# Later additions, a later read of finished chains, and new slot orders in a kernel that mixes a Fourier layer with attention

## The chip, the cores and the metric

The kernel runs on one core of one Trainium2 chip. The metric is the device time of one execution in microseconds (us); of several runs the median is taken.

## The reference

Input x is 2048 x 512 in float32. Two branches of it are mixed by a gate:

```
# Fourier branch
a, b = x @ dft_hid_re.T, x @ dft_hid_im.T
y    = dft_seq_re @ a - dft_seq_im @ b                    # 2048 x 2048 times 2048 x 512, twice
# attention branch: 32 heads of width 16
q, k, v = split(x @ wqkv)
o = softmax(q @ k.T * 16**-0.5) @ v                       # per head, 2048 x 2048 scores
out_b = o @ wo
# gate
g = sigmoid((x * gate_w).sum(-1))
out = g * y + (1 - g) * out_b
```

## The kernel before

Matrix products that need accuracy are split in a high and a low part and done as three products (high x high, high x low, low x high); this is what `h1` and `l1` mean. Heads go in pairs p = 0 to 15 (`NP`).

**Scores.** Each head's scores are computed twice. An `a` tile (`a_tile`, line 217) has queries in rows and 512 keys in columns; VectorE reduces it to row maxima (line 219, `mx`). When the maxima of half a pair (1024 queries) are complete, two deferred steps follow, one at the end of each of the next two sections: `m_parts` (lines 228 to 232: maxima negated on VectorE, split into `nhl` on GpSimd) and `m_rows` (lines 236 to 240: VectorE transposes them to `mt`, and eight small transfers, four issued on SyncE and four on GpSimd, write them as two further rows of the pair's query stack `qs`). An `s` tile (`scores`, line 682) has keys in rows and 512 queries in columns; with those rows the maximum is subtracted in the product, and ScalarE writes its exponential (line 683, `pt`). So `a` tiles run ahead of `s` tiles.

**Values.** A unit u is 128 keys of one pair and one half of the queries; there are 512 units (`UNITS`). `pv` (line 708) takes two units: eight products with `vt` (line 718, which the profile counts as sixteen instructions) into one accumulator. ScalarE copies it to `oe`, of which there are two buffers, and GpSimd adds `oe` to the running sum `osum` (lines 727 and 728; the first of a group of eight is copied straight to `osum`, line 724). After the group's last, two transfers on SyncE write the sum to `o_d` (line 731). From there `sums` (line 478), `inverse` (lines 484 to 489), `load_o` and `block` make normalised, split blocks for the projection.

**Chains.** The Fourier products and the projections are chains of products into one PSUM bank of their own (`psD`, `d` in the profile, line 378). A chain's last product has a function `after` that reads the bank: `real_next` (line 394, ScalarE copies to `y`, GpSimd splits it into `xab`), `dft_next` (lines 432 and 435, ScalarE; GpSimd adds; SyncE stores), `proj_next` (line 559 in `finish`, VectorE). `dft_next` also issues the split of a later chunk of the sequence matrix (`c_split`, lines 333 and 334 on GpSimd) and its load (line 323), in the last round of the first half reloads `xab` from `b_d` (line 428), and in the last round of all loads `wo_hl` and `o_hl` (lines 462 and 468).

**Sections.** The order of TensorE's work is written out by hand. In the long middle stretch products and scores use half the rows of the array each: a section with `half` 0 runs chain products on rows 0 to 63 and scores on rows 64 to 127, and the next section, `half` 1, the other way round; the two go through the same products, so a product is complete after both. A pattern lists a section's slots. A slot of one letter is one chain product beside one score tile of that kind on the other half. A slot of two letters has no product: the first letter is a tile on the other half, the capital one a tile on the product's half. `|` is the value product. There are three kinds:

- THIN, 26 sections, with the hidden-axis products (12 a section);
- FULL, 192 sections, with the sequence-axis products (16 a section);
- NINE, 26 sections in pairs of two different patterns, with projections (9 a section).

Before them stands a short start, after them a tail with an order of its own. The two halves have a stream of tiles each (stream 0 and stream 1).

The first product of a section that continues a chain waits, by a dependency that is added by hand, for a reader of the tiles issued since the last product of the section before: the last exponential among them, else the first reduction (`before` in `segment`).

Scores and accumulators share seven PSUM banks. `bank` gives each tile the bank that a small planner expects to be free first (`now`, `free`, `dve`, `act`; `read_by` has the costs it assumes).

**Planned steps.** `at(u, f, ...)` puts steps into `plan`, and `run_plan` issues them before the section in which unit u is reached: loads of the next pair's stacks, `sums` four units after a stack of four pairs is complete, or two units after for the last stack of three pairs, `inverse` eight or two units after that, then the blocks; `load_yg` (line 588) at 456 and 481.

## Time and profile before

| what | value |
|---|---|
| time, median of 3 runs | 1729.35 us (1729.0 to 1730.12) |
| the profiled execution's own time | 1731.44 us |
| its span, first to last instruction | 1729.6 us |
| granted TensorE clock, mean | 0.996 |
| TensorE matmul busy | 1707.6 us (99%) |
| VectorE busy | 1375.7 us (80%) |
| ScalarE busy | 1250.4 us (72%) |
| GpSimd busy | 715.1 us (41%) |

In the profile PE is TensorE's matmuls, PEld its weight loads, DVE is VectorE, ACT ScalarE, POOL GpSimd, SP SyncE, and a q behind a name means the engine's queue. A row of the waits names who waited, for whom, the total in us, how often, and the longest. A row of the chain that ended last has the start, the length and what ran; `x16` merges sixteen pieces. A row of the timeline has the start, the length, engine, line, operation, tiles and count, and in brackets the idle time before it and what ended it. Matmuls overlap and their ends are modelled, so differences of starts say more than busy times.

### The profile page before, as it was taken

What the parts mean: (1) busy time and instruction counts of PE and PEld (TensorE: products, weight loads), DVE (VectorE), ACT (ScalarE), POOL (GpSimd) and SP (SyncE); (2) the same over time, 40 slices, a digit from 0 to 9 for tenths busy, and PEclk for the clock granted to TensorE, in tenths of its full rate; (3) what the DMA queues carried; (4) which work ended last, traced back from release to release, by engine and by line L of the source; (5) the groups of instructions that cost most, each with busy time, mean ns of one, the idle gap of its engine ahead of it and who ended that gap; (6) DMA issues with size and microseconds to landing.
All of it is one profiled execution on the core that took longest, in us unless ns stands there. A gap on an engine that the chain in (4) does not pass through costs nothing.

```text
span 1729.6 us, 33828 instructions
## 1 busy us (share of the span) xinstructions
PE 1707.6 (99%) x12731; PEld 1083.8 (63%) x12731; DVE 1375.7 (80%) x2298; ACT 1250.4 (72%) x2472; POOL 715.1 (41%) x775
## 2 busy tenths in 40 slices
PE   8999999999999999999999999999999999999997
PEld 7876665656666656666666666666666666555543
DVE  5448688888888888888888888888888888799943
ACT  5211287887777778777777878778777788687885
POOL 0211144444444456444444555545554556222230
PEclk9999999999999999999999999999999999999999
DMA  8972500314141343314146535132141535450114
GB/s 283 337 167 99 164 8 8 56 32 81 38 89 49 72 110 86 78 41 81 38 93 244 101 106 111 61 71 66 52 92 52 118 99 111 181 137 8 39 29 133
DMA packets 82484, 165.12 MB, mean 95 GB/s; under 512 B 19776, under 2 KB 20032, under 8 KB 78480
## 3 DMA queue, kind: packets, MB, share of 16 engines
q1 hardware_dynamic: 77968, 162.56, 36.9%
q8 instruction: 100, 1.64, 0.4%
q0 software_dynamic: 4352, 0.39, 0.3%
q14 instruction: 64, 0.52, 0.1%
HBM read 107.73 MB, written 54.52 MB: 94 GB/s over the span
## 4 chain that ended last, share of the span: by engine, by line
PE 96%; DMA 1%; POOL 1%; DVE 1%; issue 1%; ACT 0%; SPq 0%; DVEq 0%; POOLq 0%; ACTq 0%
PE d L378 36%; PE t L718 27%; PE t L217 11%; PE t L682 11%; PE t L87 4%; PE t L88 3%; PE t L89 3%; PE t L699 1%; DMA qs<-mt 1%; POOL osum L728 0%; DVE mx L219 0%; PE t L378 0%; DMA raw<-xa_t 0%; DVE yp L559 0%; POOL qs L240 0%
## 5 line engine op out<-in xcount | busy, mean ns | idle before, releaser
L219 DVE TENSOR_REDUCE mx<-t 128x1 f32<-128x512 f32 x2048 | 1268.1, 682 | 233.8 <-PE t L217 203.5
L683 ACT ACTIVATE pt<-t 128x512 f32<-128x512 f32 x2048 | 1038.9, 633 | 19.4 <-PE t L682 12.0
L682 PE MATMUL t<-qs,ks 50*128 50x512 f32 x2048 | 750.8, 416 | 7.6 <-DMA qs<-mt 5.7
L217 PE MATMUL t<-ks,qs 48*128 48x512 f32 x2048 | 711.7, 402 | 0.1
L378 PE MATMUL d<-xab,ch 64*128 64x512 f32 x2016 | 648.8, 396 | 0.0
L728 POOL TENSOR_TENSOR osum<-osum,oe 128x512 f32<-128x512 f32 x217 | 280.4, 1292 | 671.2 <-ACT oe L727 662.6
L718 PE MATMUL t<-pt,vt 128*32 128x512 f32 x3968 | 486.5, 599 | 0.0
L378 PEld LDWEIGHTS d<-xab,ch 64*128 64x128 f32 x2016 | 366.1, 185 | 129.3 <-DVE mx L219 77.6
L682 PEld LDWEIGHTS t<-qs,ks 50*128 50x128 f32 x2048 | 367.0, 185 | 83.1 <-ACT pt L683 23.6
L378 PE MATMUL d<-xab,cl 64*128 64x512 f32 x1008 | 399.3, 396 | 0.0
L217 PEld LDWEIGHTS t<-ks,qs 48*128 48x128 f32 x2048 | 362.7, 186 | 45.1 <-DVE mx L219 19.7
L727 ACT COPY oe<-t 128x512 f32<-128x512 f32 x217 | 127.5, 587 | 260.6 <-PE t L718 258.8
L718 PEld LDWEIGHTS t<-pt,vt 128*32 128x32 f32 x3968 | 105.3, 109 | 238.1 <-issue 156.2
L378 PEld LDWEIGHTS d<-xab,cl 64*128 64x128 f32 x1008 | 185.9, 184 | 66.4 <-DVE mx L219 53.9
L334 POOL TENSOR_TENSOR cl<-craw,ch 128x512 fp32r<-128x512 f32 x126 | 162.0, 1286 | 10.2
L333 POOL CAST ch<-craw 128x512 fp32r<-128x512 f32 x126 | 77.5, 615 | 47.0 <-DMA craw<-w_seq 22.7
L83 ACT CAST hl<-t 128x512 fp32r<-128x512 f32 x48 | 28.2, 587 | 85.8 <-PE t L89 70.0
L378 PE MATMUL d<-wre,xab 64*128 64x512 f32 (+1 forms) x348 | 85.6, 391 | 0.1
L240 POOL DMA_DIRECT2D qs<-mt x128 | 72.2, 569 | 5.6 <-DVE mt L236 3.4
L378 PE MATMUL d<-wo_hl,o_hl 64*128 64x512 f32 (+1 forms) x261 | 69.6, 392 | 0.0
L378 PEld LDWEIGHTS d<-wre,xab 64*128 64x128 f32 (+1 forms) x348 | 63.9, 185 | 6.8 <-issue 1.1
L84 DVE TENSOR_TENSOR hl<-t,hl 128x512 fp32r<-128x512 f32 x48 | 32.9, 687 | 39.1 <-ACT hl L83 39.1
(115 smaller groups left out, 893.8 us busy)
## 6 DMA issues: line engine op xcount, KB each, us to landing
craw<-w_seq SPq DMA_DIRECT2D x128, 256.0 KB
qk<-hl SPq DMA_DIRECT2D x32, 512.0 KB
qs<-qk SPq DMA_DIRECT2D x96, 128.0 KB
ks<-qk SPq DMA_DIRECT2D x96, 128.0 KB
b<-hl SPq DMA_DIRECT2D x16, 512.0 KB
xab<-b SPq DMA_DIRECT2D x16, 512.0 KB
o<-osum SPq DMA_DIRECT2D x62, 128.0 KB
oh<-nh SPq DMA_DIRECT2D x12, 512.0 KB
```

The source lines that it names most:

```text
L87: nc.tensor.matmul(ps, sh, mh, start=first, stop=False)
L217: nc.tensor.matmul(ps, qs[p % 2][r, qt * P:(qt + 1) * P], ks[p % 2][r, kb * 512:(kb + 1) * 512], start=True, stop=True)
L219: user = nc.vector.tensor_reduce(mx[p % 2][:, h, qt, kb:kb + 1], ps, AX.X, ALU.max)
L240: (nc.sync, nc.gpsimd)[h].dma_start(rows.rearrange("v (q b c) -> v b q c", q=8, b=4)[:, b], mt[hf][32 * b + h:32 * b + 32:2])
L333: nc.gpsimd.tensor_copy(h1, raw)
L334: nc.gpsimd.tensor_tensor(l1, raw, h1.bitcast(F32), ALU.subtract)
L378: i = nc.tensor.matmul(self.ps, st[r], mv[r], start=not self.begun, stop=stop)
L682: nc.tensor.matmul(ps, ks[p % 2][rr, kt * P:(kt + 1) * P], qs[p % 2][rr, q0:q0 + 512], start=True, stop=True)
L683: return nc.scalar.activation(pts[u][:, 2 * qb + h], ps, AF.Exp, bias=0.0, scale=DH ** -0.5)
L718: nc.tensor.matmul(acc[32 * j:32 * j + 32], vt[:, kt, p, h:h + 32], pt[:, j], start=u == us[0], stop=u == us[-1])
L727: nc.scalar.copy(oe, acc)
L728: nc.gpsimd.tensor_tensor(o, o, oe, ALU.add)
```

## The change

1. The addition of `oe` to `osum` (and, after a group's last, the transfers to `o_d`) is put into a list by `pv` and issued at the next call of `values`, one section later, just ahead of that section's value product; in the tail at the head of the next round.
2. A section collects the `after` of a chain that it finishes and calls it behind its last tile, ahead of the value product. Before, it was called right after the chain's last product, ahead of the tile in the same slot and those behind.
3. FULL swaps its last two slots, so that it ends with an `s` tile. THIN and NINE get new orders; the number of tiles of each kind on each half, of products and of slots stays.

```
-        nc.gpsimd.tensor_tensor(o, o, oe, ALU.add)
-        if kt == NT - 1:
+        adds.append(partial(add_sum, o, oe, p, hf, kt == NT - 1))
+
+    adds = []
+
+    def add_sum(o, oe, p, hf, whole):
+        nc.gpsimd.tensor_tensor(o, o, oe, ALU.add)
+        if whole:
             for qb in range(2):
                 nc.sync.dma_start(o_d[hf][p, :, qb * 512:(qb + 1) * 512], o[64 * qb:64 * qb + 64])
+
+    def add_sums():
+        while adds:
+            adds.pop(0)()
...
-    def issue(x, half, stop=True):
+    def issue(x, half, stop=True, late=None):
...
         if stop and after:
-            after()
+            if last and late is not None:
+                late.append(after)
+            else:
+                after()
...
-    FULL = "s a s s a a s s a a s a s a s a |"
-    THIN = "sA a s a s a s s a s a s a aS |"
-    NINE = "sA s s a a sA a a s a s aS |", "aS a s s a aS sA a s a s s sA |"
+    FULL = "s a s s a a s s a a s a s a a s |"
+    THIN = "aS s a s a s a s s a s a a sA |"
+    NINE = "aS s a s a sA a a s a s sA |", "aS a s s a sA a s a s s aS sA |"
...
     def values():
...
+        add_sums()
         if us[0] < UNITS - 16:
             pv(us)
...
     def segment(pattern, half, ds, stop):
...
-        ds = iter(ds)
+        ds, late = iter(ds), []
         for slot in pattern.split():
             if slot == "|":
+                for f in late:
+                    f()
                 values()
                 continue
...
-                    i = issue(x, half, stop)
+                    i = issue(x, half, stop, late)
...
     for u in range(valued + 2, UNITS, 2):
+        add_sums()
         run_plan(u)
```

More of the change, by code (lines that the diff above doesn't have):

```diff
@@ L795, in run_plan @@
                 f()
-    FULL = "s a s s a a s s a a s a s a s a |"
-    THIN = "sA a s a s a s s a s a s a aS |"
-    NINE = "sA s s a a sA a a s a s aS |", "aS a s s a aS sA a s a s s sA |"
+    FULL = "s a s s a a s s a a s a s a a s |"
+    THIN = "aS s a s a s s a s a s a a sA |"
+    NINE = "aS s a s a sA a a s a s sA |", "aS a s s a sA a s a s s aS sA |"
     def stream(h):
```

## The prediction

> **What bounds the kernel now.** I read the busy totals first, then the chain that ended last, then the waits, then the timelines of single sections.

> ```profile
> PE 1707.6 (99%) x12731; PEld 1083.8 (63%) x12731; DVE 1375.7 (80%) x2298; ACT 1250.4 (72%) x2472; POOL 715.1 (41%) x775
> POOL osum L728 <- ACT oe L727: 662.6, 180, 10.4
> PEld d L378 <- DVE mx L219: 134.0, 159, 0.9
> PE t L682 <- DMA qs<-mt: 5.7, 2, 4.3
> ```

> TensorE is the bound: 99% busy, and nearly all of the chain. So a part of the change is worth time only where it shortens a section as TensorE sees it, from one value product (`t L718`, sixteen instructions at a section's end) to the next. The largest wait (GpSimd's additions, 662.6 us) is idle time of an engine that is 41% busy. The second (134.0 us over 159 times) looks like the target of the new slot order. The third, two waits for `qs<-mt`, is small in its own column. The chain, in order of time, shows where sections are long:

> ```profile
> 235.37 1.92 PE t L718 x16
> ...
> 370.63 2.51 PE t L718 x16
> ...
> 898.61 1.90 PE t L718 x16
> 917.94 1.85 PE t L718 x16
> 1464.05 1.85 PE t L718 x16
> 1494.73 1.85 PE t L718 x16
> 1500.55 1.85 PE t L718 x16
> ```

> An undisturbed FULL section lasts 1500.55 - 1494.73 = 5.82 us. In the THIN stretch every second value product, 13 in all, takes 2.51 instead of 1.85 to 1.92; the last of them is shown. And two places in FULL lose time: 898.61 to 917.94 is 19.33 us for three sections, 1.87 over 3 x 5.82; 1464.05 to 1494.73 is 30.68 for four (a fifth product, at 1488, is left out above), 7.40 over 4 x 5.82. Everything I credit comes from these places.

> **Part 1: THIN order, and the chain read behind the last tile.** A THIN section of the second half ends with slot `aS`; its S is the last exponential that this section's own value product needs. The chain's copy to `y` stands before it on ScalarE.

> ```profile
> 300.15 0.67 ACT L394 COPY y<-d 128x512 f32<-128x512 f32 x1
> 300.62 0.70 ACT L683 ACTIVATE pt<-t 128x512 f32<-128x512 f32 x1
> 301.37 0.14 PEld L718 LDWEIGHTS t<-pt,vt 128*32 128x32 f32 x2 [0.52 <-ACT pt L683]
> 302.35 0.18 PEld L682 LDWEIGHTS t<-qs,ks 50*128 50x128 f32 x1 [0.84 <-issue]
> ```

> The copy runs, then the exponential ends at 301.32, and the value product's last two loads follow at 301.37 after 0.52 us of idleness. The new order puts S into the first slot, and the copy moves behind the last exponential. Counting tiles: before the second THIN section stream 1 has 11 exponentials and 12 are needed; the twelfth now comes first. The wait goes whole: 13 sections x 0.655 us (2.51 less about 1.855) = **-8.5 us**. What is late next? The accumulator's bank: following the planner's sums through both orders, it is freed by the fifth reduction of the section in either, so the product's start stays. The copy moves behind the exponential, from 300.15 to about 300.63, and ends at 301.3; the next section would start at 301.70 (302.35 less 0.655), and the next chain writes its bank only in that section's second slot. So moving it costs nothing; with that cover gone it would cost up to the 0.67 us of its row a chain, 13 chains, 8.7 us.

> **Part 2: additions one section later.** The cost is in the queue behind them. `m_rows` issues half of its small transfers on GpSimd, behind the section's addition, which waits for the copy `oe` of a value product that has just ended.

> ```profile
> 906.10 0.20 DVE L236 STREAM_TRANSPOSE mt<-nhl 128x32 f32<-128x32 f32 x1
> 907.11 1.30 POOL osum L728
> 909.07 1.83 SPq L428 DMA_DIRECT2D xab<-b  x4
> 910.02 5.46 DMA qs<-mt
> 1474.71 2.55 SPq L462 DMA_DIRECT2D wo_hl<-wo  x4
> 1477.47 6.27 DMA qs<-mt
> DMA to landing us min/median/max: 1.7/1.7/6.3
> L240 POOL DMA_DIRECT2D qs<-mt x128: 561/563/644, 179.8 to 1663.6; - x128
> ```

> The transposed rows are ready at 906.30; GpSimd's four issues (0.56 each) begin after the addition, at 908.4, and the last, at 910.0, falls among 512 KB loads that SyncE began to issue at 909.07. It lands after 5.46 us instead of 1.7, and TensorE stands. The second place is the same with `wo_hl`. With the addition of the section before in that position, `oe` is long there: the issues run from about 906.4 to 908.6 and land by about 909.8 (908.1 + 1.7), at the other place by 1475.2, while the scores need them some 4 us later. Both losses go: 1.87 + 7.40 = **-9.3 us**. SyncE's own four issues are not moved. The second loss exceeds its wait because TensorE runs slowly after it:

> ```profile
> 1484.00:1490.00 6.00, 6.00 (x29) 3.44 (x33) 3.35 (x5) 2.39 (x4) 0.00 (x0) 0.52 0.02 3
> ```

> The clock column (0.52, sixth of the columns after the length) is half of full speed for six us. [...]

> What the move adds: an output copy `oe` (two buffers) now waits for an addition issued one section nearer to it. This ends on POOL rarely so far:

> ```profile
> L727 ACT COPY oe<-t 128x512 f32<-128x512 f32 x217 | 127.5, 587 | 260.6 <-PE t L718 258.8 <-POOL cl L334 1.5
> ```

> 1.5 of 260.6 us. I take zero. And a finished pair's `o` transfer is issued one section later on SyncE. For the last stack (three pairs) it now comes behind the loads of `yp`, directly ahead of the sums that read it:

> ```profile
> 1630.38 1.15 SPq L731 DMA_DIRECT2D o<-osum  x2
> 1631.89 1.76 SPq L588 DMA_DIRECT2D yp_qs<-yg  x4
> 1639.57 1.11 DVE L488 RECIPROCAL rc<-rc 48x64 f32<-48x64 f32 x2
> 1677.01 2.84 DMA o<-osum
> 1680.48 2.15 DMA rc<-o
> ```

> After the five `yp` loads (four take 1.76, so until about 1634.1) come two issues (1.15), 2.84 to land, one issue of about 0.6 and 2.15 to land: 1640.8, where VectorE wants to begin at 1639.57. VectorE stands some 1.3 us ahead of the reductions queued behind it, and TensorE waits for their banks: **+1.3 us**, bounds 0 and 2.5.

> **Part 3: FULL order.** The first product of a section waits by hand for a reader in the section before: now the reduction in slot 16, then the exponential.

> ```profile
> 906.92 4.03 ACT L683 ACTIVATE pt<-t 128x512 f32<-128x512 f32 x8
> 907.05 4.95 DVE L219 TENSOR_REDUCE mx<-t 128x1 f32<-128x512 f32 x8 [0.75 <-PE t L217]
> 911.09 0.13 PEld L718 LDWEIGHTS t<-pt,vt 128*32 128x32 f32 x4 [0.30 <-issue]
> 912.05 0.18 PEld L378 LDWEIGHTS d<-xab,ch 64*128 64x128 f32 x1 [0.84 <-DVE mx L219]
> ```

> The reductions end at 912.00, the product loads at 912.05. That reads like a wait of 0.84 on VectorE, but the THIN row at 302.35 has the same 0.84 with no reduction near. It is the value product's own end; VectorE merely ties with it. The mean of the 159 is 134.0 / 159 = 0.843, so the tie costs a few thousandths each: **-1 us** over 192 sections. The new reader ends near 911.0 (906.92 + 4.03), a us early. In the new order slot 16 still takes the bank of the fourth reduction and slot 15 that of the fifth exponential, so the pace inside is as before. Bounds: -2 and, should a bank be 0.03 late, +6.

> [...] A load done early would start the product where the value product's last quarter ends, at about 911.95 (the third quarter begins at 911.09, and a quarter takes 0.30 + 0.13) instead of 912.05: 0.10 x 192 = 19 us more. [...]

> **Part 4: NINE order.** VectorE paces these sections.

> ```profile
> 1577.41 4.98 DVE L219 TENSOR_REDUCE mx<-t 128x1 f32<-128x512 f32 x8 [0.45 <-PE t L217]
> 1580.06 0.18 PEld L682 LDWEIGHTS t<-qs,ks 50*128 50x128 f32 x1 [0.24 <-DVE mx L219]
> 1582.88 4.28 DVE L219 TENSOR_REDUCE mx<-t 128x1 f32<-128x512 f32 x7 [0.48 <-PE t L682]
> 1583.03 4.52 ACT L683 ACTIVATE pt<-t 128x512 f32<-128x512 f32 x9
> 1587.08 0.74 DVE L559 SCALAR_TENSOR_TENSOR yp<-d,omg,yp 128x512 f32<-128x512 f32 x1
> 1587.34 0.13 PEld L718 LDWEIGHTS t<-pt,vt 128*32 128x32 f32 x4 [0.30 <-issue]
> ```

> Eight reductions back to back would take 4.28 x 8 / 7 = 4.89, or 4.88 by the step of 0.60; the first row's 4.98 has 0.10 of waiting for the second tile, which moves from slot 4 to 3. The last slot waits for a bank of that sequence (0.24), so the section shortens by 0.10, 13 times: -1.3. In the other section the last reduction goes ahead of the 0.74 us step that reads the chain; the accumulator comes free about as late as the next chain writes it: 0 to 0.1, 13 times. Its S in slot 12 is the eighth exponential (seven steps of 0.48 after 1583.03 and its own 0.65), done near 1587.1, just ahead of the loads at 1587.34. **-1.0 us** in all, bounds -1.3 and +3.

> **The sum.** -8.5 - 9.3 + 1.3 - 1.0 - 1.0 = -18.5 us. The profiled execution took 1731.44 us (1729.6 of span), 2.1 over the median 1729.35 of the runs; 1712.9 there is **1711** as a median.

> **Rivals.** (a) The late transfers stay: the loads hold them wherever they are issued. For: 5.46 and 6.27 us in flight. Against: the median of 1.7, and that they would be issued 2 and 4 us earlier. Without the 9.3: 1720. Chance 0.09. (b) The THIN wait only changes its name, with a bank late by as much: 1719.5. The planner's sums speak against it. 0.07. (c) Loads come early at every border of FULL: 1692, as worked out there. 0.04. (d) Slower: in FULL, the additions, now issued behind the split of the next chunk, release `oe` late; ScalarE's copy stalls, and the exponentials behind it free slot 15's bank late. It decides once the mean delay passes 0.1 us a section (19 us over 192); at 0.15 the time is 1740. Against it: POOL's 41% and the 1.5 us above. 0.08. (e) The orders do nothing, because TensorE's own streams set every section, and the transfers stay late: 1729. 0.02. The forecast has 0.70.

> **How the numbers follow.** The unknown costs span about -4 to +8 around 1711, and the range reaches to (a) and (b): 1705 to 1721, which leaves (c), (d), (e) and tails out, some 0.18. A difference of 0.2% (3.5 us) is about what a measurement of this kernel can tell from none. Faster takes the forecast, (a), (b) and (c), less a little for errors that add up: 0.88. Same 0.03, slower 0.09.

> **What would show it.** Right: no value product of 2.51 in THIN; no TensorE wait on `qs<-mt`, all its landings near 1.7, no half clock before the tail; GpSimd's wait on `oe` nearly gone; FULL still 5.8 a section, its product's 0.84 now put down to ScalarE or to nothing; the reciprocals at L488 waiting for `rc`. Wrong: FULL above 5.9, a wait of `oe` on the additions, or `y` holding the next chain's first product.

## The result, and the profile after

| | before | after |
|---|---|---|
| time, median of 4 runs each | 1729.17 us (1727.65 to 1730.12) | 1712.55 us (1708.83 to 1713.87) |
| ratio | | 0.9901, 95% interval 0.9884 to 0.9919 |
| profiled execution, its span | 1731.44, 1729.6 us | 1713.87, 1712.1 us |

The kernel became faster by 16.6 us, 17.5 us between the two profiled spans. The forecast was 1711. One of the twelve executions of experiment 12 below took 3257 us; it counts in the median given there, but not in the ratio. The busy totals of the changed kernel, and the rows of its waits that answer to those shown of before:

```profile
PE 1693.7 (99%) x12731; PEld 1081.6 (63%) x12731; DVE 1376.3 (80%) x2298; ACT 1247.9 (73%) x2472; POOL 715.4 (42%) x775
POOL ch L333 <- PE t L682: 364.5, 73, 7.6
PEld d L378 <- issue: 150.5, 184, 1.1
POOL osum L733 <- ACT oe L727: 118.5, 58, 10.0
PE t L682 <- DMA qs<-mt: 2.4, 1, 2.4
ACT oe L727 <- POOL osum L733: 1.3, 1, 1.3
```

The addition, now line 733, waits 118.5 us instead of 662.6, and GpSimd waits for other things instead, since its work is the same. The 0.84 us ahead of a section's first product changed its name from VectorE to "issue" and kept its length. One of the two TensorE waits on `qs<-mt` is still there.

I add the time up by stages, from the start of one value product to the start of the next, since TensorE is the bound. After less before, in us:

| place | forecast | measured |
|---|---|---|
| THIN: 13 sections, 6.21 to 5.56 each | -8.5 | -8.5 |
| FULL, place near 897 (before 910) | -1.9 | -1.9 |
| FULL, place near 1465 (before 1480) | -7.4 | -1.6 |
| FULL, first section of 16 groups of eight, 5.98 to 5.82 | none | -2.6 |
| FULL, tie at each border | -1.0 | nothing seen |
| NINE, 13 sections, 5.50 to 5.35 | -1.0 | -1.9 |
| last section of NINE, 6.57 to 7.20 | none | +0.6 |
| `o` transfer of the last stack | +1.3 | 0 |
| behind the last L718, 57.25 to 55.04 | none | -2.2 (not the change's, see below) |
| everything else, some hundredths at a time | none | +0.6 |
| sum | -18.5 | -17.5 |

**THIN.** First rows of the chain, then of the timeline, of the changed kernel:

```profile
257.22 1.85 PE t L718 x16
262.79 1.85 PE t L718 x16
...
296.57 0.13 PEld L718 LDWEIGHTS t<-pt,vt 128*32 128x32 f32 x4 [0.30 <-issue]
296.89 0.69 ACT L394 COPY y<-d 128x512 f32<-128x512 f32 x1
```

No value product of 2.51 us is left; the copy to `y` runs beside the product, behind all exponentials. (A longer value product counts in the section behind it, so twelve of the 13 gains lie in the THIN stage and the last in the first FULL section.)

**The two late groups of small transfers.** At the first, the four issues of GpSimd now come at 896.85, in one piece, and TensorE doesn't wait:

```profile
896.85 2.24 POOL L240 DMA_DIRECT2D qs<-mt  x4 [3.35 <-DVE mt L236]
```

At the second only three come in one piece. The chain of waits there, and the windows behind it (sixth column behind the length: the granted clock):

```profile
1459.64 1.71 POOL qs L240 x3
1461.36 2.62 issue
1463.99 5.52 DMA qs<-mt
1469.51 0.14 issue
1469.64 0.76 PE t L682
...
1473.82 2.95 PE t L718 x16
...
1470.00:1473.00 3.00, 3.00 (x16) 2.53 (x15) 1.97 (x3) 1.56 (x3) 0.00 (x0) 0.50 0.07 25
```

GpSimd stands for 2.6 us between its third and fourth issue, waiting for nothing that the profile shows ("issue"). The fourth then falls among the `wo_hl` loads, lands after 5.52 us, TensorE is idle for 2.43 us, and the clock is halved for 6.83 us. The trace of before has the same pause, 2.0 us, and I had not seen it: the fourth issue stood alone at 1477.47, while the three ahead of it ended at 1475.47.

```profile
1473.75 1.72 POOL L240 DMA_DIRECT2D qs<-mt  x3
1477.47 0.56 POOL L240 DMA_DIRECT2D qs<-mt  x1 [2.00 <-issue]
```

### The profile page after: what moved, and what is told of

Same layout as the page of the kernel before. It is cut to its first block, busy times and chain, and to the rows that moved or that the text cites. A ratio compares the mean times of both kernels' runs of the same rounds, so it can differ in the third digit from the quotient of the medians.

```text
span 1712.1 us, 33831 instructions
## 1 busy us (share of the span) xinstructions
PE 1693.7 (99%) x12731; PEld 1081.6 (63%) x12731; DVE 1376.3 (80%) x2298; ACT 1247.9 (73%) x2472; POOL 715.4 (42%) x775
## 4 chain that ended last, share of the span: by engine, by line
PE 97%; DVE 1%; DMA 1%; issue 0%; POOL 0%; ACT 0%; SPq 0%; DVEq 0%; POOLq 0%; ACTq 0%
PE d L378 38%; PE t L718 27%; PE t L217 11%; PE t L682 9%; PE t L87 4%; PE t L88 3%; PE t L89 3%; PE t L699 1%; DVE mx L219 1%; PE t L378 0%; DMA qs<-mt 0%; DMA raw<-wqkv 0%; DVE yp L559 0%; PE t L637 0%; DMA o<-osum 0%
## 5 line engine op out<-in xcount | busy, mean ns | idle before, releaser
L219 DVE TENSOR_REDUCE mx<-t 128x1 f32<-128x512 f32 x2048 | 1267.4, 682 | 218.2 <-PE t L217 185.0
L683 ACT ACTIVATE pt<-t 128x512 f32<-128x512 f32 x2048 | 1034.9, 632 | 14.4 <-PE t L682 10.5
L682 PE MATMUL t<-qs,ks 50*128 50x512 f32 x2048 | 745.0, 414 | 3.6 <-DMA qs<-mt 2.4
L217 PE MATMUL t<-ks,qs 48*128 48x512 f32 x2048 | 695.5, 404 | 0.3 <-DVE mx L219 0.2
L378 PE MATMUL d<-xab,ch 64*128 64x512 f32 x2016 | 648.6, 396 | 0.0
L718 PE MATMUL t<-pt,vt 128*32 128x512 f32 x3968 | 478.9, 600 | 0.0
L378 PEld LDWEIGHTS d<-xab,ch 64*128 64x128 f32 x2016 | 367.1, 185 | 131.7 <-issue 90.7
L217 PEld LDWEIGHTS t<-ks,qs 48*128 48x128 f32 x2048 | 366.4, 186 | 79.0 <-DVE mx L219 26.3
L378 PE MATMUL d<-xab,cl 64*128 64x512 f32 x1008 | 399.4, 396 | 0.0
L682 PEld LDWEIGHTS t<-qs,ks 50*128 50x128 f32 x2048 | 367.6, 185 | 39.4 <-ACT pt L683 12.6
L733 POOL TENSOR_TENSOR osum<-osum,oe 128x512 f32<-128x512 f32 x217 | 278.9, 1285 | 124.4 <-ACT oe L727 118.5
L727 ACT COPY oe<-t 128x512 f32<-128x512 f32 x217 | 127.3, 587 | 254.1 <-PE t L718 252.5
L718 PEld LDWEIGHTS t<-pt,vt 128*32 128x32 f32 x3968 | 105.1, 109 | 230.2 <-issue 149.9
L378 PEld LDWEIGHTS d<-xab,cl 64*128 64x128 f32 x1008 | 186.2, 185 | 67.5 <-issue 53.6
L334 POOL TENSOR_TENSOR cl<-craw,ch 128x512 fp32r<-128x512 f32 x126 | 162.1, 1286 | 10.2
L240 POOL DMA_DIRECT2D qs<-mt x128 | 72.0, 568 | 101.5 <-DVE mt L236 94.6
L378 PE MATMUL d<-wre,xab 64*128 64x512 f32 (+1 forms) x348 | 85.5, 391 | 0.1
L378 PE MATMUL d<-wo_hl,o_hl 64*128 64x512 f32 (+1 forms) x261 | 69.7, 393 | 0.0
L378 PEld LDWEIGHTS d<-wre,xab 64*128 64x128 f32 (+1 forms) x348 | 64.0, 185 | 7.0 <-issue 1.1
```

What stands on the lines that cost most here:

```text
L217: nc.tensor.matmul(ps, qs[p % 2][r, qt * P:(qt + 1) * P], ks[p % 2][r, kb * 512:(kb + 1) * 512], start=True, stop=True)
L219: user = nc.vector.tensor_reduce(mx[p % 2][:, h, qt, kb:kb + 1], ps, AX.X, ALU.max)
L240: (nc.sync, nc.gpsimd)[h].dma_start(rows.rearrange("v (q b c) -> v b q c", q=8, b=4)[:, b], mt[hf][32 * b + h:32 * b + 32:2])
L334: nc.gpsimd.tensor_tensor(l1, raw, h1.bitcast(F32), ALU.subtract)
L378: i = nc.tensor.matmul(self.ps, st[r], mv[r], start=not self.begun, stop=stop)
L682: nc.tensor.matmul(ps, ks[p % 2][rr, kt * P:(kt + 1) * P], qs[p % 2][rr, q0:q0 + 512], start=True, stop=True)
```

## The experiments

Each kernel is the changed one, or the one before, with one edit; ratios are to the kernel before, with 95% intervals.

**1. Additions at once again** (changed kernel).

```
-        adds.append(partial(add_sum, o, oe, p, hf, kt == NT - 1))
+        add_sum(o, oe, p, hf, kt == NT - 1)
```

> The changed kernel with the additions issued at once again, all else as changed. Theory (the late additions free GpSimd for the small transfers and do nothing else): the section that lost 1.87 us near the middle of the kernel before loses about 1.9 again, and the late place near 1460 us loses about 1.6 more than in the changed kernel, so the time is 3 to 4 us above the changed kernel, near 1716. The sections at the start of each group of eight, which fell from 5.97 to 5.82, stay at 5.82. Rival (the late additions are also what shortened those sections): they go back to 5.97, 24 times 0.15, and the time is near 1720.

1716.34 us, 0.9926 (0.9911 to 0.9941), 3.8 us over the changed kernel. The section near 897 went from 5.80 back to 7.64, the one near 1465 from 10.5 to 12.1, nothing else moved by more than 0.3. So the late additions are worth these two places, and the second only 1.6 between these two executions.

**2. Old FULL order** (changed kernel).

```
-    FULL = "s a s s a a s s a a s a s a a s |"
+    FULL = "s a s s a a s s a a s a s a s a |"
```

> The changed kernel with FULL in its old order. Theory (the hand-made wait on the reduction in the last slot held back TensorE's queue, which handles further waits of the next tile only after it): the sections at the start of each group of eight go back from 5.82 to about 5.97, others stay at 5.82, and the time is 3 to 3.5 us above the changed kernel, near 1716. Rival (FULL's order is worth nothing, as its tie with the reduction suggested): no section changes, the time stays near 1712.5.

1713.39 us, 0.9911 (0.9894 to 0.9928). The first section of each group of eight went back from 5.82 to 5.98 or more. What happens at such a border, in the timelines of this kernel and then of the changed one:

```profile
392.69 0.18 PEld L378 LDWEIGHTS d<-xab,cl 64*128 64x128 f32 x1 [0.84 <-DVE mx L219]
392.88 0.18 PEld L682 LDWEIGHTS t<-qs,ks 50*128 50x128 f32 x1
```

```profile
393.81 0.18 PEld L378 LDWEIGHTS d<-xab,cl 64*128 64x128 f32 x1 [0.84 <-issue]
393.81 0.18 PEld L682 LDWEIGHTS t<-qs,ks 50*128 50x128 f32 x1
```

The first score tile on new query rows loads 0.19 us behind the product in the old order and together with it in the new one. The total hardly moved, since this execution lost 3.3 us less at the place near 1465 (sections of 8.31 and 5.80 instead of 10.5 and 6.9); experiment 6 says why.

**3. New THIN order alone** (kernel before).

```
-    THIN = "sA a s a s a s s a s a s a aS |"
+    THIN = "aS s a s a s a s s a s a a sA |"
```

> The kernel before with the new THIN pattern alone; chains are read and additions issued as before. Theory (the capital S in the first slot takes the wait out of the value product whatever stands behind it): the second of each pair of THIN sections goes from 6.21 to about 5.56, 13 times 0.65, and the time is 8 to 8.5 us below the kernel before, near 1721. Rival (the later read of the chain is what takes the wait away): a value product that still waits by 0.4 or more, and less than 3 us gained, near 1727.

1722.32 us, 0.9958 (0.9943 to 0.9972); THIN 148.59 us, as in the changed kernel (148.58; before 156.43). The order gives all of that part.

**4. The ones in sixteen transfers instead of eight** (changed kernel, L254). The theory was a count of GpSimd's transfers.

```
-            for tb in range(2):
+            for tb in range(4):
...
-                nc.gpsimd.dma_start(ks[i][64 * h + 48:64 * h + 50, tb * 2 * D:(tb + 1) * 2 * D].bitcast(F32), ones)
+                nc.gpsimd.dma_start(ks[i][64 * h + 48:64 * h + 50, tb * D:(tb + 1) * D].bitcast(F32), ones[:, :D])
```

> The changed kernel with the eight transfers of ones that GpSimd issues early on cut in two each, sixteen in all, so that every later transfer of GpSimd has a number higher by eight. Nothing else is changed. Theory (GpSimd pauses for 2 to 2.6 us before its 120th transfer, whatever runs then): the pause moves from the last transfer of the small group near 1460 us to the last one two groups earlier, near 1368 us, where no large loads run; the stall near 1464 us goes, two sections fall from 10.5 and 6.9 to 5.8 each, and the time is about 5.8 us below the changed kernel, near 1706.7. Rival (the pause belongs to the place, to the large loads that start there): it stays where it is, and the time stays near 1712.5.

1714.41 us, 0.9911 (0.9896 to 0.9926). The theory fell: eight transfers more would have moved the pause two groups. It moved by one transfer:

```profile
1459.33 1.16 POOL L240 DMA_DIRECT2D qs<-mt  x2 [0.54 <-DVE mt L236]
1463.30 1.12 POOL L240 DMA_DIRECT2D qs<-mt  x2 [2.82 <-issue]
```

**5. The ones on SyncE** (changed kernel).

```
-                nc.gpsimd.dma_start(ks[i][64 * h + 48:64 * h + 50, tb * 2 * D:(tb + 1) * 2 * D].bitcast(F32), ones)
-    load_stacks(0)
-    wos = [staged(wo[:, kt]) for kt in range(KT)]
...
+    load_stacks(0)
+    wos = [staged(wo[:, kt]) for kt in range(KT)]
...
+                nc.sync.dma_start(ks[i][64 * h + 48:64 * h + 50, tb * 2 * D:(tb + 1) * 2 * D].bitcast(F32), ones)
```

> The changed kernel, but the eight early transfers that fill rows of ones into the key tiles (L254) are issued on SyncE, behind load_stacks(0) and the four wo loads, instead of on GpSimd; nothing else differs. Theory (a store of transfer pieces on GpSimd's queue): GpSimd pauses for 2.0 to 2.8 us when it has issued a fixed amount of small pieces; in every kernel so far this was between the 119th and the 120th of its 136 transfers, and the kernel with the ones cut in sixteen moved the pause by just one transfer, so what is counted is neither transfers nor time. With the eight transfers gone the pause moves to a later transfer, some eight on (the group near 1557), the group near 1460 goes out in one piece, lands in 1.7 to 2.5 us, the section there falls from 10.5 to 5.8 and the next from 6.9 to 5.8: 5.8 us less, 1706.7 us, less whatever the pause costs at its new place (0 to 3 us). Rival 1 (the place: SyncE's or the loads' work there holds GpSimd): the pause stays before the same transfer near 1464, 1712.5 +- 2 us. Rival 2 (no count, the group is slow by the loads alone): the pause goes, but the transfers still land 5 us after issue; the section stays above 8 us, 1710 us or more.

1710.3 us, 0.9885 (0.9872 to 0.9899). The pause left its place:

```profile
1458.61 2.26 POOL L240 DMA_DIRECT2D qs<-mt  x4 [0.52 <-DVE mt L236]
1504.43 0.58 POOL L240 DMA_DIRECT2D qs<-mt  x1 [3.66 <-DVE mt L236]
1507.56 1.68 POOL L240 DMA_DIRECT2D qs<-mt  x3 [2.56 <-issue]
```

The sections near 1465 fell to 5.82 and 5.80; one near 1510 rose from 5.35 to 7.13, where the group behind the pause now met the loads of the next stack (last landing 5.74 us, TensorE idle for 1.7). Count the separate runs of data: a ones transfer has 2 (two rows), a small one 16. Ahead of the pause GpSimd had issued 8 x 2 + 111 x 16 = 1792 in the changed kernel, 16 x 2 + 110 x 16 = 1792 in experiment 4, and 113 x 16 = 1808 here, in 119, 126 and 113 transfers. It moved later by two transfers, not by the eight that I expected: the direction was right, the size not.

**6. `wo_hl` loads a quarter of a chain later** (changed kernel).

```
-            end_tiles(s // 4)
+            if s // 4 == 1:
+                end_tiles(0)
+            if s // 4 > 0:
+                end_tiles(s // 4)
```

> The changed kernel, but the four 512 KB loads into wo_hl that SyncE issues at 1462.3 to 1464.2, among the small transfers, are issued a quarter of a chain later, together with the next o_hl loads; nothing else differs. Theory (pause plus loads): GpSimd's pause before the fourth transfer stays (2.6 us), but that transfer lands 1.7 to 2.5 us after its issue instead of 5.5, so the section falls from 10.5 to about 7.5 and the next from 6.9 to 5.8: 4 us less, 1708.5 us. Rival 1 (the late landing belongs to the pause, as after a refill of the queue): landing still 5 us after issue, sections 10.5 and 6.9, 1712.5 us. Rival 2 (the moved loads meet something else): the section at the late place falls, and another one a few later grows by as much.

1710.4 us, 0.9887 (0.9871 to 0.9902). The edit came to nothing: SyncE had no other instruction between the two places, so the loads still went out at 1462.45 (1462.31 in the changed kernel). So this is another execution of the same schedule, and it came out otherwise. Chain and window:

```profile
1461.49 2.62 issue
1464.13 5.12 DMA qs<-mt
...
1471.72 1.85 PE t L721 x16
...
1470.00:1473.00 3.00, 3.00 (x31) 1.60 (x27) 2.88 (x5) 2.20 (x4) 0.00 (x0) 1.00 0.16 53
```

The transfer landed after 5.12 us instead of 5.52. TensorE was idle for 2.06 us instead of 2.43, and the clock stayed at 1.00. The two sections took 8.28 and 5.81 us, 3.3 less. In experiment 2 it was 2.07 us idle and full speed too; in the other traces with this wait, 2.43 to 4.31 us, it was half speed. That difference is probably the larger part of the 5 us by which the changed kernel's own runs scatter; only its profiled run has a trace, so this is not shown.

**7. The late read alone** (kernel before).

```
-    def issue(x, half, stop=True):
+    def issue(x, half, stop=True, late=None):
...
-            after()
+            if last and late is not None:
+                late.append(after)
+            else:
+                after()
...
+                for f in late:
+                    f()
                 values()
...
-                    i = issue(x, half, stop)
+                    i = issue(x, half, stop, late)
```

> The kernel before with one part of the change: the reader of a finished chain is issued behind the last tile of the section instead of behind the chain's last product; the slot orders and the additions stay old. Theory (the value products of the thin sections wait for the exponential of the last tile, which stands on ScalarE behind the 0.47 us copy of y): the exponential ends 0.47 us earlier, the wait shrinks from 0.66 to about 0.19 us, thirteen times: 6 us less in that stage, 1723.5 us. The kernel with the new thin order alone gave all 7.9 us of the stage, so the two parts would be two cures of one wait, not a sum. Rival (the wait is set by the slot order alone, the copy runs beside it): stage unchanged, 1729.5 us.

1722.02 us, 0.9952 (0.994 to 0.9965); THIN 150.67 us, sections of 5.72 instead of 6.21. As expected: two cures of one wait. The order alone takes it away, the read alone shortens it by 0.49 us a section, and together they give no more than the order.

**8. New FULL order alone** (kernel before).

```
-    FULL = "s a s s a a s s a a s a s a s a |"
+    FULL = "s a s s a a s s a a s a s a a s |"
```

> The kernel before with one part of the change: the new order of the full sections; everything else old. Theory (the order matters where the first score tile of a section reads new query rows, once in each group of eight): those sections fall from 5.97 to 5.82 us, about twenty times, 3 us less; the sections with late transfers keep their 7.6 and about 12 us: 1726.5 us. Rival 1 (the recorded forecast for this part, a tie of two waits of 0.02 to 0.04 us in every section): 1 us less, and the groups of eight stay as they were: 1728.5 us. Rival 2 (nothing): 1729.5 us.

1726.32 us, 0.9981 (0.9973 to 0.999), 3.1 us less. The groups of eight are back at 5.82, and the two late groups stay (7.2, and 11.4 with 6.3).

**9. Six small transfers on SyncE, two on GpSimd** (changed kernel).

```
-                (nc.sync, nc.gpsimd)[h].dma_start(rows.rearrange("v (q b c) -> v b q c", q=8, b=4)[:, b],
+                (nc.sync, nc.gpsimd)[h and b % 2].dma_start(rows.rearrange("v (q b c) -> v b q c", q=8, b=4)[:, b],
```

> The changed kernel, but of the eight small transfers of each group SyncE issues six and GpSimd two (before four and four); nothing else differs. Theory (GpSimd's queue pauses once a fixed amount of pieces has gone through it, 1792 to 1808 runs of data in the three kernels that moved it): GpSimd issues 72 instead of 136 transfers, 8 x 2 + 64 x 16 = 1040 runs, so the pause does not come at all. The section at the late place takes 5.8 us instead of 10.5 and the next one 5.8 instead of 6.9; no section of the last stage grows (the kernel with the ones on SyncE paid 1.8 us there): 1708.5 us median, 2 us less than that kernel. Price: SyncE's six transfers of 0.65 us each end 1.3 us later than four; the waits at the late place and at the one near 1507 say that a group has about 4.8 us in hand, so this stays hidden. Rival 1 (the pause belongs to the place or the time): it is still there near 1464, 1712 us. Rival 2 (the rows are needed earlier than that in some groups): sections of groups of eight grow by up to 1.3 us each, 30 us more in the worst case.

1710.95 us, 0.9893 (0.988 to 0.9906). With 1040 runs of data in all there is no pause: the late place has 5.80 and 5.83, no section grew, so the 1.3 us more on SyncE are hidden. The median is 2.5 over the forecast; behind the last L718 this execution took 56.2 us instead of 55.0, as that of experiment 11 with the same six and two did (56.3). Why is not known.

**10. `wo_hl` loads behind the next `o_hl` loads** (changed kernel).

```
-            end_tiles(s // 4)
+            if s // 4 > 0:
+                end_tiles(s // 4)
+            if s // 4 == 1:
+                end_tiles(0)
```

> The changed kernel, but the four 512 KB loads into wo_hl stand on SyncE behind the next two o_hl loads, which wait for TensorE until about 1475, so that this time they really come later; nothing else differs (the kernel that put them a quarter of a chain later in the program left them at the same place of SyncE's queue, at 1462.4). Theory (pause plus loads): GpSimd's pause of 2.6 us before the fourth transfer stays, but that transfer lands 1.7 to 2.5 us after its issue at 1464 instead of 5.1 to 5.5, before TensorE asks for it near 1467.2; sections 5.8 and 5.8, 5.8 us less than the profile of the changed kernel, 1707 to 1709 us. Rival 1 (the late landing belongs to the pause itself): landing 5 us after issue, TensorE idle for 2.0 to 2.5 us, 1710 to 1713 us. Rival 2 (the loads, now near 1476, hold the next transfers or the first projection): a later section grows by 1 us or more.

1707.25 us, 0.9875 (0.9862 to 0.9887), the fastest of all. Timeline of GpSimd and SyncE, and the landings of the small transfers from 1455 to 1520:

```profile
1458.19 1.72 POOL L240 DMA_DIRECT2D qs<-mt  x3 [0.50 <-DVE mt L236]
1462.54 0.56 POOL L240 DMA_DIRECT2D qs<-mt  x1 [2.64 <-issue]
...
1472.44 2.73 SPq L465 DMA_DIRECT2D wo_hl<-wo  x4
...
DMA to landing us min/median/max: 1.7/1.7/2.6
```

The pause is unchanged, 2.64 us. But with the four loads ten us later the fourth transfer lands at 1464.2, after 1.69 us, and the sections are 5.83 and 5.81. So the loss at this place needs both: the pause brings the transfer among the loads, the loads make it late. Between this kernel and the changed one the intervals overlap a little; the trace shows the 5.8 us, of which some 3.3 are the halved clock that experiment 6 was spared.

**11. Experiment 9, and the old order in the last section of NINE.**

```
+    LAST_NINE = NINE[0], "aS a s s a aS sA a s a s s sA |"
...
-                yield NINE, take(gen, 9)
+                yield (NINE if gen is not first or i < 4 else LAST_NINE), take(gen, 9)
```

> The changed kernel with six of eight small transfers on SyncE, as in the run beside it, and with the old order of the very last section before the tail, where no reductions are left; nothing else differs. Theory (the last section's value product waits for the exponential of its last slot, 2.0 us start to start instead of 1.3, because no reduction tile stands ahead of it): its period falls by 0.6 us, 0.6 us less than the run beside it, about 1708 us; that is too little for the ratio to show, so the section's time in the profile decides. Rival (the 0.6 us is the place, not the order): the tail stage stays at 18.1 us.

1709.16 us, 0.9885 (0.9872 to 0.9898). The value product ahead of the tail, in the chain of the changed kernel and then of this one:

```profile
1639.05 2.54 PE t L718 x16
```

```profile
1632.57 1.85 PE t L718 x16
```

The tail stage fell from 18.08 to 17.52 us: the order was it.

**12. New NINE order alone** (kernel before).

```
-    NINE = "sA s s a a sA a a s a s aS |", "aS a s s a aS sA a s a s s sA |"
+    NINE = "aS s a s a sA a a s a s sA |", "aS a s s a sA a s a s s aS sA |"
```

> The kernel before with one part of the change: the new order of the sections with nine projection products; everything else old. Theory: every second section falls from 5.50 to 5.35 us, thirteen times, 1.9 us less in that stage, and the tail stage grows by 0.6 us, where the last section's value product now waits for an exponential: 1.3 us less, 1728.1 us. The recorded forecast for this part was 1.0 us less by 0.10 us a section. Rival (the gain of that stage came from the late read or the late additions): the sections stay at 5.50 us.

1727.77 us, 0.9996 (0.9988 to 1.0005). Sections of 5.35 instead of 5.50, NINE 146.67 us instead of 148.57, the tail stage 18.06 instead of 17.48: 1.3 us by the trace, too little for the ratio.

## Why the prediction was right, and where it was not

**THIN: right, in place, cause and size.** 13 x 0.655 was forecast, 13 x 0.65 came. One thing was told too simply: the order and the late read are not two shares of the 8.5, the order has all of it (experiments 3 and 7).

**Late additions: right at the first place, mis-sized at the second.** The step that failed is "the issues run from about 906.4 to 908.6 ... at the other place by 1475.2", which took four issues of 0.56 in a row for granted at both places. At the second, GpSimd pauses between the third and the fourth, so the fourth missed its time again, and 1.6 of 7.4 us came. The prediction's lines show only the landing; GpSimd's own rows of before, shown above, would have told it: at the first place four issues in a row, at the second the last one alone at 1477.47. The 1.6 is also a difference of two executions. Over two undisturbed sections of 5.82 us, this place cost 6.0 to 7.4 us in the six traces with additions at once; with late additions and the same pause it cost 5.8 in the changed kernel and 2.5 in experiments 2 and 6, by the clock. Rival (a), "the loads hold them wherever they are issued", was half right at this place: the loads do hold a transfer that falls among them (5.5 against 1.7 us), but a transfer issued ahead of them gets through (experiment 10), as at the first place.

**The clock.** The prediction's row had half speed behind a pause of 4.3 us. Behind the waits at this place half speed lasted 3.41 us (experiments 7, 8 and 12) or 6.83 us (both kernels, experiments 1, 3 and 4), and it began between 0.9 us before the end of the wait and 0.8 us behind it. 2.43 us of idleness halved the clock, 2.06 and 2.07 at the same place did not. Whether the length of the wait decides, or something else that differed between the executions, no run tells apart. A price by the length of the wait alone is off by up to 3.3 us here.

**`o` transfer of the last stack, +1.3: did not come.** Timeline of SyncE and VectorE in the changed kernel:

```profile
1609.87 1.75 SPq L588 DMA_DIRECT2D yp_qs<-yg  x4
...
1614.81 1.15 SPq L736 DMA_DIRECT2D o<-osum  x2
1617.77 1.24 SPq L478 DMA_DIRECT2D rc<-o  x2
...
1623.86 1.11 DVE L488 RECIPROCAL rc<-rc 48x64 f32<-48x64 f32 x2
```

I had kept the `yp` loads at the time that they had before, 1631.89. But that time was itself set by the `o` transfer standing ahead of them on SyncE, which waited there 10.7 us for GpSimd's last addition. Moved behind them, it no longer holds them, and both are early: the reciprocals wait for nothing.

**FULL: right that the pace stays, wrong on where the gain is.** A section still takes 5.82 us, and the tie of some thousandths in each of 192 was not to be seen. The gain is 0.16 us in 16 sections, where the first score tile stands on new rows. That the order decides it is shown (2 and 8); by what means is not shown: the two timelines give only the 0.19 us by which that tile's load stands behind the product's in the old order.

**NINE: the wait was the right one, its size a little low.** The eight reductions now take 4.87 us, the 4.88 that was worked out (before 4.98):

```profile
1585.15 4.87 DVE L219 TENSOR_REDUCE mx<-t 128x1 f32<-128x512 f32 x8 [0.42 <-PE t L682]
```

The section gained 0.15 rather than 0.10. Before, the last tile of each of the 13 sections waited for VectorE, 0.23 to 0.29 us. Now one of them does, 0.12 us, and in nine a tile near the end waits for ScalarE instead, 0.12 to 0.17 us. So VectorE no longer sets the end of this section, and its 0.11 us are not the measure of the gain. Its last pair was not looked at: there reductions have run out, nothing stands ahead of the exponential in slot 12, and the value product waits for it (0.6 us, experiment 11).

**Behind the last L718, -2.2: chance, not a gain.** Chain of before, then of the changed kernel:

```profile
1683.90 0.50 PE t L682 x2
1684.40 3.54 PE t L699 x16
```

```profile
1661.71 2.36 DMA o<-osum
...
1664.71 2.02 DMA rc<-o
...
1668.01 0.50 PE t L682 x2
1668.50 1.85 PE t L699 x16
```

The two transfers took 2.84 and 2.15 us before, 0.61 us more, and the value product behind them then ran at half speed, 1.69 us more; that is all of it. But it belongs to this one execution. The kernels of experiments 3, 7, 8 and 12 are the one before with an edit elsewhere, and their traces have 55.0 to 55.4 us in this stretch and 1.85 us for that value product. It fits that the profiled execution of before was 2.1 us over its median, which the forecast took off without knowing where it lay. Why the transfers were longer in it is not known.

Of the rivals, (b), (c) and (e) are out: the thin wait went, no load at a border comes early (0.84 us, as before; what an early one would give was an estimate, and no run shows it), and every order gave something. (d) is out too: `oe` waited for an addition once, 1.3 us.

So the total was right partly by luck. Misses cancelled: 5.8 us at one place and the tie's 1.0 did not come, 0.6 was not foreseen and 0.6 is scattered, against 2.6 + 0.9 + 1.3 us gained beyond the forecast. That leaves 15.3 us for the change between the two traces; the other 2.2 are the slow end of the execution of before. The medians are 16.6 apart, since the changed kernel's profiled execution was itself 1.3 us over its median.

## What to carry to other kernels

Before a transfer is credited with coming early, look at each of its issues in the trace, not at the first: a gap with no releaser between two issues moved along with them here (2.0 us before, 2.6 after). When an instruction is moved behind another on its queue, work out the other's new time as well, since it may have waited only for the one that moved. And if a small transfer has to land in time, keep large loads of another queue behind it; here four loads issued ten microseconds later were worth more than the additions (5.3 us between the medians, against 3.8). Last, compare a stage with the same stage of other executions before a difference is put down to the change: 2.2 us here were an accident of one trace.

## What the runs showed of the hardware

**GpSimd paused once between two issues.** In each of twelve traces, when 1792 to 1808 separate runs of data had gone out (counted as in experiment 5), the next issue came 2.0 to 2.8 us late, at the three different transfers at which the kernels reach that count; in the two traces with 1040 in all none did. What GpSimd does in that time, and why it was 2.0 us with additions at once and 2.6 to 2.8 with late ones, no run shows.

**A small transfer among large ones took three to nearly four times as long.** 2 KB landed after 1.7 us alone, after 5.1 to 6.3 us beside four loads of 512 KB.
